# Moving the second batch's bucket products and value halves, and loading two weight chunks into an idle buffer

## The chip, the cores and the metric

The kernel runs on one core of one Trainium2 chip. Its engines are TensorE (PE, with its weight loads PEld), VectorE (DVE), ScalarE (ACT), GpSimd (POOL) and SyncE (SP), which issues nearly all transfers. The metric is the device time of one launch in microseconds (us); lower is better.

## The reference

Hash-bucketed attention is followed by two feed-forward layers.

- Attention: batch 2, 8 heads, 768 positions, head width 64. Six signs of a projection give each query and key a bucket number; a query attends only to keys of its own bucket: `softmax(where(q_bucket == k_bucket, q @ k.T / 8, -1e9)) @ v`.
- First layer, on 1536 tokens of width 512: `h = x @ w_in` (512 to 2048), `g = where(h > 0, h, exp(min(h, 0)) - 1)`, `x = g @ w_out` (2048 to 512).
- Second layer: `h = x @ w_in2`, `g = s * max(h, 0)**2 + b`, `out = g @ w_out2`, of the same sizes.

The weights arrive as 64-bit floats, the inputs of attention as 32-bit floats.

## The kernel before

**Precision.** Products run on 16-bit pairs: each operand is split into a high half and a low half (the rest), and a product is three matmuls: high by high, high by low, low by high.

**Weights of the first layer.** `w_stream` is a generator that works on chunks of 512 KB raw 64-bit data. A step of it does four things: it finishes the chunk that was joined one step before (L188 on ACT writes the high half, L204 on DVE or L202 on POOL the low half), joins the oldest loaded chunk from its two 32-bit words into a float (L194, L195, L197 on DVE), and issues the load of the next chunk (L167, on SP's queue) into one of three raw buffers. A join waits until two chunks are in `loaded`, so a chunk is loaded two steps before it is joined; 16 chunks need 19 steps. `w_in` is streamed in the first loop of attention (L823), one step a yield from unit 2 on. `w_out` gets its own generator behind it (L844); it is stepped by `w1_step` in the loop over the first layer's slots (two slots of three, L873). Its chunks come by column group: four for each of the four 128-column groups of `w_out`. Before unit 40's scores the stream has to be through: `att_step` drains it (L860). At its end its buffers are given to attention.

**Attention** is 96 units (batch, 128 queries, head): 48 of each batch. A unit is: scores on PE (L358), clamp and row minimum on DVE (L368), exponential on ACT (L370), then a split into halves (L389 on ACT, L392 on POOL), a transposing transfer `pt<-ph` on SP's queue (L394), and the product with the values on PE (L412), some four units later. Eight units make a chunk of 128 tokens, which `u_norm` writes to the input `xx` of the first layer. `xx` is three tiles of four chunks: `xx[1]` first gets data behind unit 39.

**Set-up of batch 1.** Heads go in pairs `hp` 0 to 3. While units 41 to 54 run, four functions are called at steps written out by hand (`sched`, by unit number): `p_split` (halves of k and q and their transposes) at unit 41 + 2 hp, `p_bits` (signs: 20 matmuls L320, then L323 on DVE) three units later, `p_buck` (four matmuls L333, then four activations L337 that write the bucket part of k and q) one unit after that. `p_v` splits the values: L303 on ACT, L304 on DVE. The first scores of pair `hp` in batch 1 are unit 48 + 2 hp, and the first product with its values is that unit's L412.

**Order.** The program text gives priorities. From them and its own timeline of the engines the framework's planner writes one fixed order for each engine and each queue, in which the chip executes. The first layer's products (L531) lie between attention's steps. It runs in blocks of 256 tokens: `up` 16 slots (`h`), `down` 16 slots (`x2p`). The second layer (`h` again, then `y` L775) follows when attention is over.

Of the kernel before, what the change touches and what calls it, by code (L numbers as in the profile page):

```python
# [10 lines left out]
I32 = mybir.dt.int32  # L11
# [30 lines left out]
WST = 2  # L42
LOAD1 = [30, 41, 42, 44]
LOADV1 = [46, 46, 48, 48]
PV1 = [48, 49, 50, 52]

GUEST = [(0, "k"), (0, "q"), (2, "k"), (2, "q"), (0, "v"), (1, "v")]
NS = 2
# [13 lines left out]
SC_N = 16  # L62
PRE = 4
W_FROM = 2
LN2 = 0.6931471805599453


def model_kernel(tc, q, k, v, proj, w_in, w_out, w_in2, w_out2, s2, b2, sel, pop, eye, out):
    nc = tc.nc
# [23 lines left out]
    with ExitStack() as base:  # L93
# [50 lines left out]
        def w_raw(st):  # L144
            return pool(st, "wraw", WRAW, side="right")


        def w_tiles(p, nm):
            return [p.tile([128, KF, 512], F16, name=f"{nm}{x}") for x in "hl"]

        def w_in_chunks(dst, dram):
            w = dram.bitcast(I32)
            return [((lambda a, f=f: dst(f)) if callable(dst) else [d[:, f, :] for d in dst], w[:, 256 * f:256 * f + 256].rearrange("(k p) n -> p k n", p=128))
                    for f in range(KF)]

        def w_col_chunks(dst, dram):
            w = dram.bitcast(I32)
            return [([z[:, f:f + 4, 128 * d:128 * d + 128] for z in dst],
                     w[128 * f:128 * f + 512, 256 * d:256 * d + 256].rearrange("(k p) n -> p k n", p=128))
                    for d in range(KM) for f in range(0, KF, 4)]  # L160

        def w_load(ch, wraw):
            t = wraw.tile([128, 512, 2], I32, tag="w", name="wraw")
            o = t.rearrange("p n t -> p (n t)")
            if len(ch[1].shape) == 3:
                o = o.rearrange("p (k n) -> p k n", k=ch[1].shape[1])
            nc.sync.dma_start(out=o, in_=ch[1])  # L167
            return t

        def w_stream(chunks, wraw, words, delay=0, aside=0):  # L170
            loaded, joined = [], []
            for n_, ch in enumerate(chunks + [None] * 3):
                with late_by(delay):
                    done = joined.pop(0) if joined else None
                    if done:
                        (dst, _), w = done
                        w = w.bitcast(F32)
                        if callable(dst):
                            dst = dst(w)
                            done = dst and (None, w)  # L180
                    if done:
                        hi, lo = dst
                        if len(hi.shape) == 3:
                            w = w.rearrange("p (k n) -> p k n", k=hi.shape[1])
                        aside_ = n_ - 3 < aside
                        if aside_:
                            nc.gpsimd.tensor_scalar(w, w, SW, None, op0=ALU.mult)
                        nc.scalar.activation(out=hi, in_=w, func=ACTF.Copy, scale=1.0 if aside_ else SW)  # L188
                    if len(loaded) == 2 or (ch is None and loaded):
                        c0, t = loaded.pop(0)  # L190
                        a, x = words()
                        a, x = a.bitcast(I32), x.bitcast(I32)
                        low, top = t[:, :, 0], t[:, :, 1]
                        nc.vector.tensor_scalar(x, top, 3, 0x3FFFFFFF, op0=ALU.logical_shift_left, op1=ALU.bitwise_and)  # L194
                        nc.vector.scalar_tensor_tensor(out=x, in0=low, scalar=29, in1=x,  # L195
                                                       op0=ALU.logical_shift_right, op1=ALU.bitwise_or)
                        nc.vector.scalar_tensor_tensor(out=a, in0=top, scalar=-0x40000000, in1=x,  # L197
                                                       op0=ALU.bitwise_and, op1=ALU.bitwise_or)
                        joined.append((c0, a))
                    if done:  # L200
                        if aside_:
                            nc.gpsimd.tensor_tensor(out=lo, in0=w, in1=hi, op=ALU.subtract)  # L202
                        else:
                            nc.vector.scalar_tensor_tensor(out=lo, in0=w, scalar=SW, in1=hi,  # L204
                                                           op0=ALU.mult, op1=ALU.subtract)
                    if ch is not None:
                        loaded.append((ch, w_load(ch, wraw)))
                yield
# [153 lines left out]
        def u_soft(u):  # L362
# [5 lines left out]
            nc.vector.tensor_scalar(f, sps.pop(u), CLAMP, None, op0=ALU.min, op1=ALU.min, accum_out=mx)  # L368
            (nc.gpsimd if U0 <= u < MXP else nc.vector).tensor_scalar(mx, mx, sm / (SQ * SQ), 10.0 * LN2, op0=ALU.mult, op1=ALU.add)  # L369
            nc.scalar.activation(out=f, in_=f, func=ACTF.Exp, scale=-sm / (SQ * SQ), bias=mx,  # L370
# [44 lines left out]
        xx = [xs_.tile([128, 2 * KM, 512], F16, name=f"x{i}") for i in range(B * C // 4)]  # L415
# [28 lines left out]
        def at(step, fn, *a):  # L444
            sched.setdefault(step, []).append((fn, a))
# [10 lines left out]
        for hp in range(HP):  # L456
            at(PV0 + hp, p_v, 0, hp)
            e1 = (C - 1) * H + 2 * hp + 1
            at(LOAD1[hp], p_load, 1, hp, "k")
            at(LOAD1[hp], p_load, 1, hp, "q")  # L460
            at(e1, p_split, 1, hp, "k", "act")
            at(e1, p_split, 1, hp, "q", "act")
            at(e1 + 3, p_bits, 1, hp)
            at(e1 + 4, p_buck, 1, hp)
            at(LOADV1[hp], p_load, 1, hp, "v")
            at(PV1[hp], p_v, 1, hp)
        done_chunks = [0]
        in_done = [0]
        nxt = {"s": 0, "av": 0, "soft": [], "split": [], "lag": LAG0}
# [339 lines left out]
        if True:  # L809
# [3 lines left out]
            for hp, nm in ((0, "k"), (0, "q"), (1, "k"), (1, "q")):  # L813
# [5 lines left out]
            wdec = w_raw(wdst), lambda: (wst.tile([128, 512], F32, tag="wa", name="wa"),  # L819
                                         ring.take("w", [128, 512], F32, "wx"))  # L820
            ws1 = w_stream(w_in_chunks(wi, w_in), *wdec, aside=ASIDE)
            n = 0
            for _ in att:  # L823
                n += 1
                if nxt["s"] >= W_FROM and n % WN == 0:
                    next(ws1, None)
                if done_chunks[0] == BLOCKS1[0]:
                    break
# [12 lines left out]
                gp[0] = pool(gst1, "gp1", 1)  # L841

            wo = w_tiles(wop, "wo")
            ws1 = chain(ws1, w_stream(w_col_chunks(wo, w_out), *wdec))  # L844
            live = {"w1": True, "att": True}
            credit = 0.0

# [24 lines left out]
            for ks, cost in enumerate(moe1(wi, wo, gp, next_gp, tmp, tmpg, att_step)):  # L872
# [7 lines left out]
                if not live["att"] and ws2 is None:  # L880
                    exst.close()
                    ast.close()
                    ps_y = pool(pst, "ps_y", Y2, space=PSUM)
                    lp = right(late, "late", 1)
                    tmp2.append(right(late, "tmp2", 3))
                    wraw = w_raw(wlate)
                    wjp = right(wlate, "wjoin", 1)
                    sbt = lp.tile([128, 2], F32, name="sbt")
                    sbs = const.tile([128, 3], F32, name="sbs")
                    nc.sync.dma_start(out=sbt[:, 0:1], in_=s2.rearrange("(o t) -> o t", o=1).to_broadcast([128, 1]))  # L890
                    nc.sync.dma_start(out=sbt[:, 1:2], in_=b2.rearrange("(o t) -> o t", o=1).to_broadcast([128, 1]))
                    nc.vector.tensor_scalar(sbs[:, 0:1], sbt[:, 0:1], UN * SG2, None, op0=ALU.mult)
                    nc.vector.tensor_scalar(sbs[:, 1:2], sbt[:, 1:2], SG2, None, op0=ALU.mult)
                    nc.vector.tensor_scalar(sbs[:, 2:3], sbt[:, 1:2], 2.0 * SG2, None, op0=ALU.mult)
                    sb["s"], sb["b"], sb["2b"] = (sbs[:, x:x + 1] for x in range(3))
                    wq = []
                    co = wo_chunks(w_out2, wq, wjp)
                    ci = w_in_chunks(wi2_new, w_in2)
                    ch = ci[:W2PRE]
                    for f in range(KF):  # L900
                        ch += ci[W2PRE + f:W2PRE + f + 1] + co[f:f + 1]
                    ws2 = w_stream(ch, wraw,
                                   lambda: (wjp.tile([128, 512], F32, tag="wa", name="wa", bufs=4),
                                            ps_x.tile([128, 512], F32, tag="x", name="wx")), delay=D2)
                elif ws2 is not None and W2EV(ks) and fed2[0] < W2PRE + 3:
                    next(ws2)
                    fed2[0] += 1
# [72 lines left out]
```

## Time and profile before

| | |
|---|---|
| median of 3 runs | 716.36 us (713.94 to 717.16) |
| profiled execution: time, span | 715.27 us, 713.5 us |
| mean granted TensorE clock | 0.986 of full speed |
| chunks of `w_out` finished | 16, from 108.8 to 179.9 us |
| set-up of batch 1 | 180.6 to 248.5 us |

The share of the chain of work that ended last is 59% PE, 11% transfers, 10% ACT, 7% DVE. Read the profile by stretches: an engine's share over the whole span mixes a first part, in which attention's dependencies set the pace, with a second in which PE has no idle time. A wait's row names what came last.

### The profile page before, as it was taken

How to read it: one execution, taken by the hardware profiler on the slowest of the kernel's cores; microseconds unless marked ns; L12 is line 12 of the kernel's file. 1: busy time of each engine (PE TensorE's matmuls, PEld its weight loads, DVE VectorE, ACT ScalarE, POOL GpSimd, SP SyncE). 2: the span in 40 equal slices, each digit the busy share in tenths (PEclk: the TensorE clock that was granted, in tenths of full speed). 3: DMA queues.
4: the chain of work that ended last, by engine and by line, in shares of the span. 5: the costliest groups of instructions: out<-in, count | busy, mean ns of one | idle time of the engine just before them, and what ended most of it. 6: DMA issues, size and time to landing. Idle time of an engine off the chain costs nothing.

```text
span 713.5 us, 15214 instructions
## 1 busy us (share of the span) xinstructions
PE 659.6 (92%) x6192; PEld 504.0 (71%) x6192; DVE 516.6 (72%) x885; ACT 417.2 (58%) x687; POOL 272.7 (38%) x219
## 2 busy tenths in 40 slices
PE   2789869888887999999999999999999999999998
PEld 0368657676666777888888988874444446888887
DVE  5688899888878468645744699439999726999730
ACT  2897679874797887756755333234555525555520
POOL 1257778873445278945854421311211200000000
PEclk9999979999999999999999999999999999999999
DMA  9984599999899588966768545004453000000100
GB/s 234 259 222 135 159 223 225 205 229 219 178 208 215 88 142 159 154 119 123 123 112 120 132 153 175 1 25 125 121 149 115 0 1 1 16 30 32 45 30 30
DMA packets 206742, 89.73 MB, mean 126 GB/s; under 512 B 171856, under 2 KB 203344, under 8 KB 206672
## 3 DMA queue, kind: packets, MB, share of 16 engines
q1 hardware_dynamic: 206080, 88.63, 56.4%
q8 instruction: 48, 0.79, 0.5%
q10 hardware_dynamic: 592, 0.14, 0.1%
q14 instruction: 22, 0.18, 0.1%
HBM read 43.13 MB, written 3.15 MB: 65 GB/s over the span
## 4 chain that ended last, share of the span: by engine, by line
PE 59%; DMA 11%; ACT 10%; DVE 7%; issue 6%; POOL 5%; SPq 0%; DVEq 0%; ACTq 0%; POOLq 0%
PE h L531 24%; PE y L775 15%; PE x2p L531 10%; DMA pt<-ph 6%; PE s L358 4%; POOL ph L392 3%; ACT p L370 3%; PE xacc L412 3%; ACT ph L389 2%; PE xacc L406 1%; DVE e L546 1%; DMA k<-src 1%; ACT gh L551 1%; PE pT L379 1%; DVE p L368 1%
## 5 line engine op out<-in xcount | busy, mean ns | idle before, releaser
L392 POOL TENSOR_TENSOR ph<-p,ph 128x768 f16<-128x768 f32 x80 | 133.9, 1679 | 65.3 <-ACT ph L389 45.7
L531 PE MATMUL h<-x,wih 128*128 128x256 f16 x768 | 132.5, 276 | 0.1
L531 PE MATMUL h<-x,wi 128*128 128x512 f16 x576 | 124.5, 379 | 0.0
L368 DVE TENSOR_SCALAR_CACHE_REDUCE p<-s 128x768 f32<-128x768 f32 x96 | 91.0, 950 | 44.4 <-PE s L358 42.1
L370 ACT ACTIVATE p<-p,mx 128x768 f32<-128x768 f32 x96 | 89.1, 928 | 46.4 <-DVE mx L369 40.5
L775 PE MATMUL y<-wqh,a 128*128 128x256 f16 x672 | 110.3, 273 | 0.0
L775 PEld LDWEIGHTS <-a 128*128 128x128 f16 x1008 | 98.5, 98 | 11.8
L531 PE MATMUL x2p<-gh,woh 128*128 128x256 f16 x384 | 104.8, 274 | 2.0 <-ACT woh L188 1.0
L531 PE MATMUL x2p<-gh,wol 128*128 128x256 f16 x384 | 105.0, 274 | 1.5 <-DVE wol L204 1.5
L531 PE MATMUL h<-x,wil 128*128 128x256 f16 x384 | 106.0, 276 | 0.0
L531 PE MATMUL x2p<-gl,woh 128*128 128x256 f16 x384 | 104.9, 274 | 0.5 <-POOL gl L554 0.4
L531 PEld LDWEIGHTS <-wi 128*128 128x128 f16 x576 | 56.3, 98 | 67.8
L775 PE MATMUL y<-wql,a 128*128 128x256 f16 x336 | 91.2, 273 | 0.0
L358 PE MATMUL s<-k,q 128*128 128x512 f16 (+1 forms) x384 | 81.0, 336 | 4.8 <-DVE p L368 4.5
L531 PEld LDWEIGHTS <-woh 128*128 128x128 f16 x768 | 74.8, 98 | 13.5 <-ACT woh L188 1.4
L531 PEld LDWEIGHTS <-wih 128*128 128x128 f16 x768 | 75.2, 99 | 12.8 <-issue 0.5
L554 POOL TENSOR_TENSOR gl<-g,gh 128x512 f16<-128x512 f32 x48 | 58.1, 1211 | 63.3 <-ACT gh L551 62.7
L412 PE MATMUL xacc<-vv,pt 128*128 128x64 f16 x1440 | 57.7, 195 | 18.2 <-DMA pt<-ph 18.2
L412 PEld LDWEIGHTS <-pt 128*128 128x128 f16 x1440 | 53.9, 99 | 24.3 <-DMA pt<-ph 21.2
L389 ACT ACTIVATE ph<-p 128x768 f16<-128x768 f32 x80 | 66.6, 836 | 5.2 <-DMA pt<-ph 4.1
L567 DVE SCALAR_TENSOR_TENSOR g<-h,sbs,r 128x512 f32<-128x512 f32 x48 | 35.7, 745 | 23.6 <-ACT r L564 23.6
L564 ACT ACTIVATE r<-h 128x512 f32<-128x512 f32 x48 | 28.2, 590 | 39.5 <-PE h L531 39.5
(121 smaller groups left out, 1043.3 us busy)
## 6 DMA issues: line engine op xcount, KB each, us to landing
wraw<-in_moe_w_in SPq DMA_DIRECT2D x32, 512.0 KB, 3.8
wraw<-in_moe_w_out SPq DMA_DIRECT2D x32, 512.0 KB, 3.9
out<-y SPq DMA_DIRECT2D x10, 256.0 KB, 2.0
raw<-in_k SPq DMA_DIRECT2D x6, 384.0 KB, 4.4
raw<-in_q SPq DMA_DIRECT2D x6, 384.0 KB, 4.4
v<-in_v SPq DMA_DIRECT2D x4, 384.0 KB, 5.1
pt<-ph SPq DMA_TRANSPOSE x80, 4.0
x<-in_k SPq DMA_DIRECT2D x2, 384.0 KB, 5.0
```

Of the source, the lines that this page charges most:

```text
L358: nc.tensor.matmul(p[:, a0:a1], w[b, hp][:, j, c, :], kf[:, a0:a1], start=(x == 0), stop=(x == 1))
L368: nc.vector.tensor_scalar(f, sps.pop(u), CLAMP, None, op0=ALU.min, op1=ALU.min, accum_out=mx)
L370: nc.scalar.activation(out=f, in_=f, func=ACTF.Exp, scale=-sm / (SQ * SQ), bias=mx, accum_out=sums[b, c][:, h:h + 1])
L379: nc.tensor.transpose(p[:, 128 * cc:128 * cc + 128], f[:, 128 * cc:128 * cc + 128], ident)
L389: nc.scalar.activation(out=t[:, 0, :], in_=f, func=ACTF.Copy)
L392: nc.gpsimd.tensor_tensor(out=t[:, 1, :], in0=f, in1=t[:, 0, :], op=ALU.subtract)
L412: nc.tensor.matmul(acc, o[:, C * x + cc, :], vv[:, j, cc, y, :], start=(z == 0 and cc == 0), stop=(z == 2 and cc == C - 1))
L531: nc.tensor.matmul(p, ws[a](kk), xs[b](kk), start=(kk == 0 and z == 0), stop=(kk == n_kk - 1 and z == 2))
L554: nc.gpsimd.tensor_tensor(out=gl, in0=t["g"], in1=gh, op=ALU.subtract)
L564: nc.scalar.activation(out=t["r"], in_=p, func=ACTF.Relu, scale=UN)
L567: nc.vector.scalar_tensor_tensor(out=g, in0=p, scalar=sb["s"], in1=t["r"], op0=ALU.mult, op1=ALU.mult)
L775: nc.tensor.matmul(p, a[:, xa, kk, :], wq[y][:, WQ[n], kk, :], start=first and k == 0, stop=k == 3 * K2 - 1, skip_group_check=True)
```

## The change

Four things change: `BUCK1`, a new constant, puts `p_buck` of batch 1 two units behind `p_bits`, not one. `PV1` calls `p_v` of pairs 1 to 3 at units 50, 52 and 54, not 49, 50 and 52; pair 0 stays at 48. In the first loop of attention the raw data of the first two chunks of `w_out` is loaded into `xx[1]`, at units 6 and 8 (one tile of `xx` holds just two raw chunks). The stream of `w_out` then starts with these two in `loaded`: its first step joins at once, and it has 17 steps, not 19. Since `wo` does not exist yet when the early loads are issued, the chunks' destinations become functions.

```diff
-PV1 = [48, 49, 50, 52]
+PV1 = [48, 50, 52, 54]
+BUCK1 = 5
+EARLY = [6, 8]
...
+        def w_early(ch, x):
+            t = xx[1].rearrange("p a t -> p (a t)").bitcast(I32)[:, 1024 * x:1024 * x + 1024]
+            nc.sync.dma_start(out=t.rearrange("p (k n) -> p k n", k=ch[1].shape[1]), in_=ch[1])
+            return ch, t.rearrange("p (n t) -> p n t", t=2)
+
-        def w_stream(chunks, wraw, words, delay=0, aside=0):
-            loaded, joined = [], []
+        def w_stream(chunks, wraw, words, delay=0, aside=0, loaded=(), late_dst=False):
+            loaded, joined = list(loaded), []
...
+                        if late_dst:
+                            dst = dst()
...
-            at(e1 + 4, p_buck, 1, hp)
+            at(e1 + BUCK1, p_buck, 1, hp)
...
-            n = 0
+            n, early = 0, []
+            co1 = w_col_chunks(lambda: wo, w_out)
             for _ in att:
                 n += 1
+                if len(early) < len(EARLY) and nxt["s"] >= EARLY[len(early)]:
+                    early.append(w_early(co1[len(early)], len(early)))
...
-            ws1 = chain(ws1, w_stream(w_col_chunks(wo, w_out), *wdec))
+            ws1 = chain(ws1, w_stream(co1[len(early):], *wdec, loaded=early, late_dst=True))
```

## Rows read from the trace of the kernel before

**Rows 1.** The page: busy time of each engine over the span.
```profile
PE 659.6 (92%) x6192; PEld 504.0 (71%) x6192; DVE 516.6 (72%) x885; ACT 417.2 (58%) x687; POOL 272.7 (38%) x219
```
**Rows 2.** Busy time by stretches; first columns: stretch, its length.
```profile
core 0: us, PE busy (x) PEld busy (x) DVE busy (x) ACT busy (x) POOL busy (x), PEclk, DMA share, GB/s
...
100.00:162.00 62.00, 56.27 (x679) 46.31 (x678) 55.09 (x98) 51.02 (x93) 48.62 (x47) 0.96 1.07 225
162.00:181.00 19.00, 16.47 (x203) 13.50 (x202) 15.88 (x26) 7.83 (x13) 5.13 (x4) 1.00 0.92 217
181.00:245.00 64.00, 54.62 (x617) 42.07 (x616) 47.08 (x83) 52.59 (x87) 30.89 (x23) 0.97 0.91 176
...
300.00:445.00 145.00, 144.49 (x1657) 125.96 (x1656) 93.10 (x182) 76.78 (x130) 70.05 (x50) 1.00 0.65 133
```
**Rows 3.** PE's waits, 165 to 185 us: total, times, longest.
```profile
PE x2p L531 <- DVE wol L204: 1.5, 3, 0.9
PE x2p L531 <- ACT woh L188: 1.0, 2, 0.7
```
**Rows 4.** DVE's instructions by line, 162 to 181 us: busy, mean ns, idle before.
```profile
L204 DVE SCALAR_TENSOR_TENSOR wol<-wa,woh 128x512 f16<-128x512 f32 x6 | 5.2, 871 | 2.8 <-ACT woh L188 2.8
L194 DVE TENSOR_SCALAR wx<-wraw 128x512 int32<-128x512 int32 x5 | 3.5, 693 | 0.1
```
**Rows 5.** SP's queue in order of time, two places: start, length.
```profile
41.33 18.10 SPq L167 DMA_DIRECT2D wraw<-in_moe_w_in  x4
...
98.07 0.38 SPq L167 DMA_DIRECT2D wraw<-in_moe_w_out  x1
```
**Rows 6.** Busy time by stretches, 40 to 60 us.
```profile
40.00:60.00 20.00, 17.67 (x140) 14.56 (x140) 15.25 (x32) 17.25 (x28) 11.24 (x9) 0.91 0.58 187
```
**Rows 7.** PE's waits, 185 to 250 us.
```profile
PE xacc L412 <- DMA pt<-ph: 5.1, 6, 1.3
PE pone L333 <- DVE bits L323: 2.3, 1, 2.3
```
**Rows 8.** All engines in order of time, around pair 2's bucket products.
```profile
226.73 3.27 DVE L304 SCALAR_TENSOR_TENSOR vv<-x,vv 128x768 f16<-128x768 f32 x2
226.97 4.53 POOL L392 TENSOR_TENSOR ph<-p,ph 128x768 f16<-128x768 f32 x2 [0.49 <-ACT ph L389]
...
229.93 0.94 DVE L323 TENSOR_SCALAR bits<-pbit 128x768 f16<-128x768 f32 x1
...
230.93 0.80 PE L333 MATMUL pone<-bits,sel_sb 128*128 128x512 f16 x2 [2.33 <-DVE bits L323]
```
**Rows 9.** Busy time by stretches, 231 to 234.2 us.
```profile
231.00:234.20 3.20, 3.20 (x14) 1.91 (x14) 2.39 (x6) 0.73 (x1) 0.50 (x1) 0.50 1.09 133
```
**Rows 10.** DVE in order of time: clamps of units 45, 46, 51 and 52.
```profile
194.50 0.94 DVE L368 TENSOR_SCALAR_CACHE_REDUCE p<-s 128x768 f32<-128x768 f32 x1
...
208.49 0.95 DVE L368 TENSOR_SCALAR_CACHE_REDUCE p<-s 128x768 f32<-128x768 f32 x1
...
241.40 0.95 DVE L368 TENSOR_SCALAR_CACHE_REDUCE p<-s 128x768 f32<-128x768 f32 x1
...
248.07 0.96 DVE L368 TENSOR_SCALAR_CACHE_REDUCE p<-s 128x768 f32<-128x768 f32 x1 [0.70 <-PE s L358]
```
**Rows 11.** ACT in order of time: last bucket activations of pairs 0 and 3.
```profile
205.77 1.80 ACT L337 ACTIVATE q<-pone,pop_sb 64x768 f16<-64x768 f32 x2
...
246.67 1.80 ACT L337 ACTIVATE q<-pone,pop_sb 64x768 f16<-64x768 f32 x2
```
**Rows 12.** PE in order of time: scores of units 48 and 54.
```profile
219.49 0.81 PE L358 MATMUL s<-k,q 128*128 128x512 f16 x4
...
250.36 0.81 PE L358 MATMUL s<-k,q 128*128 128x512 f16 x4
```
**Rows 13.** Tile vv, 185 to 250 us: least, median, greatest ns.
```profile
L304 DVE SCALAR_TENSOR_TENSOR vv<-x,vv x2: 958/1679/2400, 226.7 to 227.6; 128x768 f16<-128x768 f32 x2
L304 DVE SCALAR_TENSOR_TENSOR vv<-raw,vv x2: 957/958/958, 232.4 to 239.7; 128x768 f16<-128x768 f32 x2
```

More of the change, by code (lines that the diff above doesn't have):

```diff
@@ L157, in w_col_chunks @@
             w = dram.bitcast(I32)
-            return [([z[:, f:f + 4, 128 * d:128 * d + 128] for z in dst],
+            return [((lambda d=d, f=f: [z[:, f:f + 4, 128 * d:128 * d + 128] for z in dst()]),
                      w[128 * f:128 * f + 512, 256 * d:256 * d + 256].rearrange("(k p) n -> p k n", p=128))
```

## The prediction

> **What bounds the kernel now.** I read the page's busy shares first, then stretches, then PE's waits in the stretches that the change touches, then the order of time around them. PE is busy 92% of the span [rows 1], and the stretches show where the rest lies: from 300 to 445 us it is idle 0.5 of 145 us, so nothing is to be had there from an earlier attention. From 100 to 162 us it is idle 5.7 of 62 us, from 162 to 181 us 2.5 of 19, from 181 to 245 us 9.4 of 64 [rows 2]. PE's work is the same after the change, so the change is worth the idle time and slow clock that it takes out of these three stretches, or puts in.
>
> In the first of them DVE is the fullest engine beside PE: 55.1 of 62 us. In the second the picture turns: DVE 15.9 of 19, ACT 7.8, POOL 5.1 [rows 2]. That is the drain of `w_out`'s stream ahead of unit 40's scores: five chunks are joined one behind the other (five of L194, and five each of its two companions L195 and L197; six of L204), with 2.8 us of waiting for ACT's high half inside [rows 4]. Attention stands still meanwhile. In the third, attention starts batch 1, in long chains over all engines, and PE's fixed order runs into them.
>
> **The early loads.** They remove no work: 16 chunks are loaded, joined and split as before. Two loads move from just before the stretch at 100 us, where the second of them is issued at 98.07, to units 6 and 8, that is into the time when SP itself sat 18.1 us over four loads, waiting for raw buffers [rows 5]. The early loads wait for no buffer, but they stand in SP's queue behind such a load, and what is queued behind them (the next `w_in` loads, the transposes of the first chunks of `xx`) starts one issue later. An issue takes 0.38 us [rows 5], so two cost at most 0.8 us if all of it fell on the path; transfers are at a share of 0.58 from 40 to 60 us [rows 6], so the data fits beside the rest. I take 0 and keep 0 to +0.8 for the range.
>
> What they do change is the stream's start: the first join comes in step 1, not step 3. Every chunk is finished two steps sooner in the program, three slots of the first layer. Where the drain starts, 13 chunks are done instead of 11, and three are left instead of five. A chunk costs DVE three joins of 0.69 us (the row of L194; three instructions alike) and 0.69 to 0.87 us of L204 [rows 4], about 2.8 us; so the drain loses 5.6 us of DVE time, which turns up between 100 and 162 us. There DVE has 6.9 us idle [rows 2], so it fits at best wholly into gaps, at worst not at all, and attention enters the drain between 0 and 5.6 us later and leaves it between 5.6 and 0 us earlier than now. PE's own gain is smaller. In the drain PE has products to do and stops only for the weights themselves: 1.5 + 1.0 = 2.5 us [rows 3]. With three chunks less to wait for (the last column group is needed at slot 28, and its last chunk comes at slot 25 instead of 28 in the program's order) these waits go. What is late next is attention's restart, which PE reaches 2.5 us sooner: the gain holds if attention leaves the drain at least 2.5 us earlier, about the middle of the 0 to 5.6 us above. I take **-2.5 us**, with ends -2.5 (all kept) and 0 (handed on to the first transposes of batch 1).
>
> **Bucket products one unit later, value halves one or two units later.** No instruction is added. Of the 64 us from 181 on I look at the one long wait of PE that these functions make: pair 2's bucket product waits 2.33 us for its signs. The signs (L323) stood on DVE behind two value halves (L304), which took 3.27 us together [rows 8]. With `p_v` of pair 1 at unit 50, at least one of these two is behind the signs, and with `p_buck` a unit later the product comes into PE's order when its signs are ready. So 2.3 us go [rows 7], **-2.3**. The wait has a tail: right behind it the granted clock is 0.50, the lower level of 1.2 GHz, over 3.2 us [rows 9], which costs PE half of 3.2 us, **-1.6**.
>
> Against that stands what waits for the bucket activations: the scores of the same pair. Now pair 0's last activation ends at 205.77 + 1.80 = 207.57 us [rows 11] and its first scores (unit 48) start at 219.49 [rows 12], a margin of 11.9 us. A unit later is 14.0 us there (clamps of units 45 and 46 at 194.50 and 208.49 [rows 10]), so PE would wait 2.1 us. Pair 3 ends at 248.47 [rows 11] and unit 54 starts at 250.36 [rows 12], a margin of 1.9; a unit there is 6.7 us (units 51 and 52 at 241.40 and 248.07 [rows 10]), which would be a wait of 4.8 us. Bounds for this new wait: 0 if the planner finds first-layer products to put before the scores, 2.1 + 4.8 = 6.9 us if it finds none. I take **+2.1**: pair 0's unit is long whatever the change does, whereas pair 3's unit is long because of the chain in [rows 8] that gets shorter, and `down` products are there to fill it.
>
> The three moved value halves have their readers from unit 50 on, some four units behind the scores, and their raw data lies in buffers that nothing else wants in batch 1; I cost the move itself at 0. If that cover were gone, one ACT and one DVE instruction of 0.96 us [rows 13] would stand before a product, under 2 us. One of the four L304 took 2.40 us and the others 0.96 [rows 13], the long one beside two splits on POOL of 4.53 us together [rows 8]. The Trainium skill (SBUF — State Buffer, Who interferes with whom) says that a VectorE instruction with two inputs in SBUF and a GpSimd instruction that reads SBUF shut each other out of a shared port; the row agrees. By that rule three moved halves could each lose or gain 2.40 - 0.96 = 1.44 us of DVE time, by where they land beside POOL's splits; the sum here takes none of it.
>
> **Sum.** -2.5 - 2.3 - 1.6 + 2.1 = -4.3 us. The profiled execution took 715.27 us (its span 713.5 and 1.8 around it), so 711.0; the median of the runs shown is 716.36, 1.1 above it, which gives **712.1 us** as a median. A measurement of this kernel can tell about 0.5%, 3.6 us: faster begins at 712.8, slower at 719.9.
>
> **The rivals.**
>
> *The waits move on.* PE's order is fixed against a chain of transfers: six waits for the transposes `pt<-ph`, 5.1 us, stand in the same stretch [rows 7]. If attention leaves the drain no earlier, each us saved in front of one of these comes back behind it: 716.4 us, give or take 2. For it speaks that DVE's work from 100 to 181 us is the same sum; against it that DVE waited idle inside the drain for 2.8 us [rows 4], a loss that shrinks with it.
>
> *More than the named waits.* If attention does restart 5.6 us earlier, the planner's order for batch 1 has that much more slack, and other idle time of the 9.4 us goes too. Half of what is left beyond the 2.3 already counted is 3.5 us: with -2.5 - 2.3 - 1.6 and no new wait this is -9.9, 705.4 in the profile and 706.5 as a median. For it speaks that this stretch has the most idle time after 100 us; against it that its chains are latencies, which an earlier start alone doesn't shorten.
>
> *The late bucket.* The scores take over the wait: pair 0 and pair 3 both lose their margin, 6.9 us, and behind the second wait the clock falls as in [rows 9], 1.6 us more; in return -3.9 as above, and the drain's 2.5 us are eaten by the wait behind it. 715.27 - 3.9 + 6.9 + 1.6 = 719.9, or 721.0 as a median. It decides from the point where the activations end later than the planner's place for the scores by more than 1.9 us in pair 3. For it speaks that this margin is smaller than any unit in the stretch; against it that the planner sees this dependency and reorders.
>
> That the change doesn't do what it says can be ruled out for the loads' number, but the planner may leave a moved step where it was; this is part of the first rival.
>
> **How the numbers follow.** Forecast 0.42, waits move on 0.18, more than the named waits 0.16, late bucket 0.24. The forecast's own range is 709 to 716 (its median 712.1, with the drain's gain at 0 to the upper side and the new wait at 0 or 4.8 to either). It counts as faster in 0.72 of its cases and as the same in the rest: 0.30 and 0.12. The second rival is wholly faster, 0.16; the first the same in 0.13, faster in 0.01, slower in 0.04; the late bucket slower in 0.20, the same in 0.04. Together: faster 0.47, same 0.29, slower 0.24. The range goes from below the second rival's 706.5 to the late bucket's 721.0: 705 to 721, with the 0.8 us of the early issues inside.
>
> **What would show it.** Right: two loads of `w_out` between 41 and 85 us; three chunks back to back in the drain and no wait of `x2p` for `woh` or `wol` over 0.5 us; attention's first split of batch 1 before 178 us instead of 181; no wait of L333 over 1 us and no stretch at 0.50 between 200 and 250 us; a new wait of L358 for L337 of about 2 us. Wrong: DVE idle from 100 to 162 us still near 6.9 us although its work grew (then attention was pushed, not filled); PE's idle time from 181 to 245 us at 9 us or more; or a wait of L358 for L337 over 4 us.

## The result: slower by 1.1%, and the profile after

The changed kernel takes 722.24 us (median of 4 runs, 720.71 to 723.46) where the kernel before, run beside it, takes 715.25 (4 runs). The ratio on record is 1.0114, with a 95% interval of 1.0083 to 1.0145; the quotient of the two medians, 1.0098, lies inside it. The forecast was 712.1 us and its range went from 705 to 721. The profiled execution took 723.46 us, 8.2 more than that of before.

First the page's busy line, against [rows 1]. The kernel's lines have moved: those from L187 to L820 of before stand 9 further down here (the low half L204 is now L213, its counterpart on POOL L202 is L211, the multiply L187 is L196, the signs' product L333 is L342).

```profile
PE 665.2 (92%) x6192; PEld 507.9 (70%) x6192; DVE 516.8 (72%) x883; ACT 417.6 (58%) x687; POOL 275.0 (38%) x223
```

The counts hold the surprise. The prediction had "They remove no work" of the early loads and "No instruction is added" of the rest. DVE has 883 where it had 885, and POOL 223 where it had 219: two instructions have left DVE and four have come to POOL. The groups of POOL between 100 and 185 us show which (line, engine, operation, tiles, count, then busy us, mean ns, idle us before them):

```profile
L196 POOL TENSOR_SCALAR wa<-wa 128x512 f32<-128x512 f32 x2 | 3.0, 1488 | 0.2
L211 POOL TENSOR_TENSOR wol<-wa,woh 128x512 f16<-128x512 f32 x2 | 2.3, 1159 | 0.2
```

Two chunks of `w_out` are now split by way of POOL: POOL multiplies the joined words (L196), ACT makes the high half from the product, and POOL subtracts (L211). Before, no chunk of `w_out` went that way. The reason stands in one line of `w_stream` that the diff does not touch: `aside_ = n_ - 3 < aside`, with `n_` the stream's step. It means "the first `aside` chunks go over POOL"; `w_in` asks for some, and `w_out` for none, `aside=0`. A chunk used to be finished in step 3 at the earliest (steps count from 0), so `n_ - 3` began at 0. With two chunks loaded beforehand, the first two are finished in steps 1 and 2; `n_ - 3` is -2 and -1, which is less than 0, and both take the detour.

The stretches, against [rows 2] (us; busy time and instructions of PE, PEld, DVE, ACT, POOL; granted TensorE clock, DMA share, GB/s):

```profile
100.00:162.00 62.00, 54.77 (x639) 43.96 (x637) 57.59 (x92) 50.54 (x90) 49.02 (x46) 0.94 0.98 202
162.00:181.00 19.00, 18.59 (x223) 14.85 (x221) 17.99 (x27) 10.99 (x19) 10.35 (x10) 0.94 1.11 226
181.00:245.00 64.00, 56.08 (x568) 43.09 (x572) 44.13 (x83) 48.86 (x82) 25.14 (x21) 0.89 0.94 180
245.00:300.00 55.00, 51.11 (x653) 41.89 (x653) 35.51 (x78) 42.75 (x75) 39.41 (x27) 1.00 0.83 137
300.00:445.00 145.00, 144.66 (x1683) 126.04 (x1681) 90.85 (x182) 79.83 (x136) 74.16 (x52) 1.00 0.66 130
```

The fourth stretch is not among [rows 2]; before it was

```profile
245.00:300.00 55.00, 53.36 (x671) 44.61 (x670) 39.50 (x86) 45.67 (x82) 42.40 (x29) 1.00 0.90 146
```

PE's idle time has hardly changed in sum: 7.2 us in the first stretch (5.7 before), 0.4 in the second (2.5), 7.9 in the third (9.4), 3.9 in the fourth (1.6). The clock has: 0.94, 0.94 and 0.89 in the first three (0.96, 1.00 and 0.97 before). I took all stretches of one us from 40 to 320 us and added up two things: PE's idle time, and its busy time multiplied by what the granted clock is short of full speed. Before they are 30.8 and 8.1 us, after 31.6 and 15.9. The sum grows by 8.6 us, about the 8.2 of the two executions, and nearly all of it is clock. That isn't one execution's accident: the mean granted clock is 0.969 to 0.976 in all four executions of the changed kernel, and 0.973 to 0.993, on average 0.984, in those of the kernel before that ran beside the experiments (one of 984 us, far out of line, is left out here and in the ratios).

Not all of the 8.2 us need be the change's, though. A part is there by 65 us, long before the detour. The clamp of unit 10 (units count from 0), before, after, and in experiment e6 below:

```profile
62.21 0.96 DVE L368 TENSOR_SCALAR_CACHE_REDUCE p<-s 128x768 f32<-128x768 f32 x1 [0.31 <-PE s L358]
...
64.85 0.96 DVE L377 TENSOR_SCALAR_CACHE_REDUCE p<-s 128x768 f32<-128x768 f32 x1 [0.37 <-PE s L367]
...
67.06 0.96 DVE L377 TENSOR_SCALAR_CACHE_REDUCE p<-s 128x768 f32<-128x768 f32 x1 [0.37 <-PE s L367]
```

After is 2.6 us late there. But e6 runs the order of before on PE, DVE, ACT and POOL up to 170 us and is 4.9 us late, and e2, with that order up to 195 us, is 2.4 us early (59.78). Executions of one order differ that much, so the 2.6 us may belong to this execution; single profiles below are to be read with this in mind.

Three pairs of stretches show how the clock comes in, the wait and what follows it (columns as above; in the second and third pair the two overlap):

```profile
144.00:147.00 3.00, 0.64 (x20) 0.63 (x20) 3.00 (x6) 1.20 (x3) 2.70 (x3) 1.00 1.25 233
147.00:151.00 4.00, 4.00 (x35) 2.46 (x32) 4.00 (x10) 3.70 (x8) 3.45 (x3) 0.57 1.23 185
...
188.00:193.00 5.00, 2.00 (x27) 1.16 (x25) 3.62 (x9) 5.00 (x10) 3.03 (x3) 0.85 1.03 192
191.00:199.00 8.00, 7.08 (x62) 4.44 (x60) 7.56 (x14) 6.27 (x12) 5.71 (x5) 0.57 1.08 234
...
212.00:215.00 3.00, 0.39 (x7) 0.11 (x6) 0.69 (x1) 2.06 (x5) 1.15 (x1) 1.00 1.38 147
214.00:219.00 5.00, 4.10 (x34) 2.96 (x35) 3.36 (x6) 3.10 (x6) 3.86 (x4) 0.66 1.11 217
```

Each time PE first runs 0.4 to 2.0 us in 3 to 5, and then works, with under 1 us of idle time, through 4 to 8 us whose mean clock is 0.57 or 0.66: most of it is at the lower level (0.5, which is 1.2 GHz). PE's waits, in the same order, are 2.36 us for a transpose, 2.08 for the transfer `k<-src` with 0.92 for `x` behind it, and 2.61 for a transpose.

### The profile page after: what moved, and what is told of

Same layout as the page of the kernel before. It is cut to its first block, busy times and chain, and to the rows that moved or that the text cites. A ratio compares the mean times of both kernels' runs of the same rounds, so it can differ in the third digit from the quotient of the medians.

```text
span 721.7 us, 15215 instructions
## 1 busy us (share of the span) xinstructions
PE 665.2 (92%) x6192; PEld 507.9 (70%) x6192; DVE 516.8 (72%) x883; ACT 417.6 (58%) x687; POOL 275.0 (38%) x223
## 4 chain that ended last, share of the span: by engine, by line
PE 58%; DMA 8%; DVE 7%; issue 3%; ACT 3%; POOL 2%; SPq 0%; DVEq 0%; ACTq 0%; POOLq 0%
PE h L540 25%; PE y L784 15%; PE x2p L540 11%; DMA pt<-ph 6%; PE s L367 3%; PE xacc L421 3%; DVE p L377 1%; DVE e L555 1%; POOL ph L401 1%; ACT ph L398 1%; DVE wol L213 1%; DVE g L557 1%; DVE wa L206 1%; POOL gl L563 1%; ACT gh L560 1%
## 5 line engine op out<-in xcount | busy, mean ns | idle before, releaser
L401 POOL TENSOR_TENSOR ph<-p,ph 128x768 f16<-128x768 f32 x80 | 132.2, 1656 | 78.2 <-ACT ph L398 53.5
L540 PE MATMUL h<-x,wih 128*128 128x256 f16 x768 | 135.2, 278 | 1.0 <-DVE x L633 0.9
L377 DVE TENSOR_SCALAR_CACHE_REDUCE p<-s 128x768 f32<-128x768 f32 x96 | 91.1, 952 | 45.6 <-PE s L367 42.0
L367 PE MATMUL s<-k,q 128*128 128x512 f16 (+1 forms) x384 | 83.3, 343 | 5.0 <-DVE p L377 4.0
L421 PE MATMUL xacc<-vv,pt 128*128 128x64 f16 x1440 | 59.2, 196 | 21.0 <-DMA pt<-ph 21.0
L367 PEld LDWEIGHTS <-q 128*128 128x128 f16 x384 | 35.4, 102 | 24.0 <-issue 9.5
```

What stands on the lines that cost most here:

```text
L367: nc.tensor.matmul(p[:, a0:a1], w[b, hp][:, j, c, :], kf[:, a0:a1], start=(x == 0), stop=(x == 1))
L401: nc.gpsimd.tensor_tensor(out=t[:, 1, :], in0=f, in1=t[:, 0, :], op=ALU.subtract)
L421: nc.tensor.matmul(acc, o[:, C * x + cc, :], vv[:, j, cc, y, :], start=(z == 0 and cc == 0), stop=(z == 2 and cc == C - 1))
L540: nc.tensor.matmul(p, ws[a](kk), xs[b](kk), start=(kk == 0 and z == 0), stop=(kk == n_kk - 1 and z == 2))
```

## The experiments

All were timed in five rounds against the kernel before, which ran beside them at 713.8 to 714.4 us. Ratios are to that; brackets hold the 95% interval.

**e1, the early loads alone.**

```diff
-PV1 = [48, 50, 52, 54]
-BUCK1 = 5
+PV1 = [48, 49, 50, 52]
+BUCK1 = 4
 EARLY = [6, 8]
```

> The early loads alone, with the old places of the bucket products and value halves. The traces of before and after reach the same amount of matmul work 3.8 us apart at 185 us and 8.2 us apart at the end. Theory 1 (the early stream costs before the set-up of batch 1, the late buckets behind it): +3.8 us against before, about 719 us. Rival 2 (all of it is the early stream, and the rest only its echo in batch 1): +7 to +8, about 723. Rival 3 (all of it is the late buckets): 0, about 715.

Measured: 721.11 us, 1.0096 [1.0064, 1.0127]. The loads with what hangs on them are enough for nearly all of the loss.

**e2, the late functions alone** (`EARLY = []`, the rest as changed).

> The late bucket products and value halves alone, without early loads. Theory 1: the part behind 185 us, +4.4 us, about 719.7. Rival 2: 0 within 1 us. Rival 3: +7 to +8, about 723. The forecast on record had this part at -1.8 us (-2.3 -1.6 +2.1), about 713.5.

Measured: 717.11 us, 1.0037 [1.0013, 1.006]. A loss where the prediction saw -3.9 and +2.1.

**e3, the early loads without the detour**, and **e4, the whole change without it.**

```diff
-                        aside_ = n_ - 3 < aside
+                        aside_ = bool(aside) and n_ - 3 < aside
```

> As the early loads alone, but the first two chunks of w_out are finished by DVE as in before. In the changed kernel they go through GpSimd (a multiply and a subtraction each), because the test for it counts steps from the stream's start and the stream now starts two steps further on. Theory 4 (that detour, 5.3 us of GpSimd work and low halves on DVE that take 1.45 us beside it instead of 0.85, is what the early stream costs after 100 us): what remains is the 2.6 us lost by 60 us, of which little is left at 134 us: 0 to +2.6 us against before, 715 to 718. Rival 5 (the loads themselves, or the joins two steps sooner, are the cost): the same as the early loads alone, within 1 us.

> The whole change, with the first two chunks of w_out finished by DVE as in before. Theory 4 with theory 1: the late part's +4.4 us and at most 2.6 of the early one: 719 to 722. Rival 5: as the changed kernel, 722. If the forecast on record failed by the detour alone: 711 to 713.

Measured: e3 715.33 us, 1.0014 [0.9994, 1.0035]; e4 714.05 us, 0.9995 [0.9972, 1.0017]. The detour makes 5.8 us of e1's time (721.11 - 715.33) and 8.2 of the change's (722.24 - 714.05; these two ran in different rounds, and each against its own kernel before they are 7.2 apart). Without it the change is worth nothing.

**e5, the detour alone**, in the kernel before: `aside` becomes a set of chunks, and `w_out`'s chunks 0 and 1 are in it. Nothing is loaded early or moved. **e6, the same detour elsewhere:** chunks 12 and 13, in the drain.

```diff
-                        aside_ = n_ - 3 < aside
+                        aside_ = n_ - 3 in aside
...
-            ws1 = chain(ws1, w_stream(w_col_chunks(wo, w_out), *wdec))
+            ws1 = chain(ws1, w_stream(co1[len(early):], *wdec, aside=(0, 1), loaded=early, late_dst=True))
```

> The kernel before, with nothing of the change but the detour: chunks 0 and 1 of w_out are finished over GpSimd (multiply and subtraction). No early loads, the stream has its 19 steps. Theory 4 (the detour is the cost: 5.3 us of work on a GpSimd that is busy 48.6 of 62 us there, in front of the splits that attention's row buffers wait for): +5 to +7 us against before, as far as the early loads alone lie above those finished by DVE (5.8). Rival 6 (the detour costs only together with the stream that starts two steps sooner, or the reshuffled order does): 0 to +2.

> The kernel before with the same detour for chunks 12 and 13 instead, which are finished in the drain ahead of unit 40, where GpSimd is busy 5.1 of 19 us. Theory 4: no cost, -1.5 to +1 us against before. Rival 6 (any reshuffling of the planned order costs some us): +3 to +6, here as for chunks 0 and 1.

Measured: e5 719.09 us, 1.006 [1.0037, 1.0084]; e6 714.70 us, 1.0008 [0.9982, 1.0034]. The same four instructions on POOL cost 4.3 us (0.6% of 714.35) among attention's splits and nothing that can be measured in the drain. What happens among the splits is seen at POOL's queue in the changed kernel (start us, us, engine, line, operation, tiles):

```profile
110.97 1.49 POOL L196 TENSOR_SCALAR wa<-wa 128x512 f32<-128x512 f32 x1
112.54 1.69 POOL L401 TENSOR_TENSOR ph<-p,ph 128x768 f16<-128x768 f32 x1
...
117.43 1.49 POOL L196 TENSOR_SCALAR wa<-wa 128x512 f32<-128x512 f32 x1
119.00 1.16 POOL L211 TENSOR_TENSOR wol<-wa,woh 128x512 f16<-128x512 f32 x1
120.51 1.65 POOL L401 TENSOR_TENSOR ph<-p,ph 128x768 f16<-128x768 f32 x1
...
123.96 1.16 POOL L211 TENSOR_TENSOR wol<-wa,woh 128x512 f16<-128x512 f32 x1
```

L401 is attention's split. From a chunk's multiply to its subtraction pass 8.0 us for the first chunk and 6.5 for the second: weights and attention take turns in one queue. DVE at the same time:

```profile
116.26 0.96 DVE L377 TENSOR_SCALAR_CACHE_REDUCE p<-s 128x768 f32<-128x768 f32 x1
...
120.19 0.69 DVE L206 SCALAR_TENSOR_TENSOR wa<-wraw,wx 128x512 int32<-128x512 int32 x1 [1.07 <-POOL wol L211]
...
126.39 2.00 DVE L213 SCALAR_TENSOR_TENSOR wol<-wa,woh 128x512 f16<-128x512 f32 x1
...
128.91 0.94 DVE L377 TENSOR_SCALAR_CACHE_REDUCE p<-s 128x768 f32<-128x768 f32 x1
```

The join of the third chunk (L206) waits 1.07 us until POOL's subtraction gives one of the two joined buffers free. And the two clamps (L377), those of units 26 and 27, are 12.65 us apart. In the kernel before the same two are 7.28 us apart:

```profile
113.80 0.95 DVE L368 TENSOR_SCALAR_CACHE_REDUCE p<-s 128x768 f32<-128x768 f32 x1
...
121.08 0.95 DVE L368 TENSOR_SCALAR_CACHE_REDUCE p<-s 128x768 f32<-128x768 f32 x1
```

In e1, e5 and e9 (below) the gap is 12.7, 12.7 and 11.1 us, in e3 and e6 6.5 and 7.2. Waiting is the smaller part of the longer gap: DVE is idle 2.27 us in it (0.78 before). It also has 12 instructions to run between the two clamps where it had 8. Unit 27's clamp stands further back in the order that the planner wrote around POOL's new work.

**e7, the bucket products alone** (`EARLY = []`, `BUCK1 = 5`, `PV1` as before), and **e8, the values alone** (`EARLY = []`, `BUCK1 = 4`, the new `PV1`).

> The bucket products one unit later, the value halves at their old places. The late part as a whole gave +2.6 us (0.37%). If the buckets are what costs in it: +2.6, 1 to 4. If it is the value halves: 0 within 1 us.

> The value halves of pairs 1 to 3 later, the bucket products at their old place. The planned order differs from before's in a few instructions of DVE and ACT and between PE's matmuls alone. If the buckets are what costs in the late part: 0 within 1 us; the forecast on record would have it take away the 2.3 us wait of the third pair's product and the clock behind it, -2 to -4. If the value halves cost: +1 to +4.

Measured: e7 717.26 us, 1.0043 [1.0021, 1.0066]; e8 713.87 us, 0.9996 [0.9971, 1.0021].

e8 tells less than it was meant to, since the planner left the values where they were. By operation and tile, the order on PE, DVE, ACT and POOL is that of the kernel before. Both value halves still run ahead of pair 2's signs (L332):

```profile
226.43 3.28 DVE L313 SCALAR_TENSOR_TENSOR vv<-x,vv 128x768 f16<-128x768 f32 x2
229.63 0.94 DVE L332 TENSOR_SCALAR bits<-pbit 128x768 f16<-128x768 f32 x1
```

and PE still waits 2.4 us for the signs. The new `PV1` makes no difference between e7 and e2 either: both run one order (sign products aside, which run side by side on PE). So they are two measurements of it, and the loss of both is the bucket products'. In e7, the matmuls around pair 2's product show it, against [rows 8] and [rows 9] (in square brackets: idle us before it, and what ended that):

```profile
233.73 0.27 PE L540 MATMUL x2p<-gl,woh 128*128 128x256 f16 x1 [2.73 <-POOL gl L563]
...
234.95 0.67 PE L342 MATMUL pone<-bits,sel_sb 128*128 128x512 f16 x2 [0.62 <-DVE p L377]
```

and the stretch behind:

```profile
235.00:238.50 3.50, 3.50 (x17) 2.42 (x17) 0.08 (x1) 3.39 (x6) 0.40 (x1) 0.52 1.01 202
```

The product's own wait fell from 2.33 to 0.62 us. Right ahead of it a product of the first layer now waits 2.73 us for POOL, and the stretch behind is at 0.52: wait and slow clock are still there, under another name. But they only replace what was there before, and so they aren't e7's loss. Its stretches:

```profile
181.00:245.00 64.00, 54.44 (x602) 41.95 (x600) 47.33 (x85) 51.73 (x86) 30.12 (x23) 0.97 0.93 178
245.00:300.00 55.00, 53.00 (x683) 44.22 (x679) 38.28 (x81) 44.60 (x78) 41.28 (x28) 1.00 0.82 140
300.00:445.00 145.00, 143.17 (x1643) 124.78 (x1642) 93.27 (x183) 77.49 (x132) 69.65 (x49) 1.00 0.63 131
```

PE is idle 9.6 us in the first (9.4 before, at the same clock), and 3.8 in the other two together (2.1 before); in e2 it is 9.5 and 4.0. What the late products cost shows up behind the set-up of batch 1.

**e9, the multiply alone:** chunks 0 and 1 are multiplied on POOL as in e5, but DVE makes the low half.

```diff
-                        if aside_:
+                        if aside_ and not late_dst:
                             nc.gpsimd.tensor_tensor(out=lo, in0=w, in1=hi, op=ALU.subtract)
+                        elif aside_:
+                            nc.vector.scalar_tensor_tensor(out=lo, in0=w, scalar=1.0, in1=hi,
+                                                           op0=ALU.mult, op1=ALU.subtract)
```

> The kernel before with half of the detour: chunks 0 and 1 of w_out are multiplied on GpSimd (2 x 1.49 us of the 5.3), and their low halves are written by DVE. If the detour costs by GpSimd's time in front of attention's splits: its share, 4.3 x 3.0 / 5.3 = +2.4 us against before. If it costs because DVE's next join waits for GpSimd's subtraction to free the joined buffer (1.1 us in the traces): 0 to +1.

Measured: 719.22 us, 1.007 [1.0039, 1.0102]. The two subtractions, 2.3 us of POOL, add nothing that can be seen; two multiplies are enough for e5's whole loss. Its profile can't say where: of the 5.9 us by which this execution is behind, 4.2 are there at unit 10's clamp (66.45 us), ahead of the multiplies.

**e10, loads that nobody reads:** two loads of the early loads' size into `xx[1]` at units 6 and 8; the stream of `w_out` stays as before.

> The kernel before, plus the two early loads into the idle tile of xx at units 6 and 8, whose data nobody reads: the stream loads the same chunks again in its own time, with 19 steps and no detour. It is the price of the two early transfers alone. If they are hidden, as the forecast on record had it: 0 to +0.8 us. If the 2.6 us by which the changed kernel is behind at 60 us are theirs: +1.5 to +3.

Measured: 713.99 us, 0.9997 [0.9975, 1.002].

**e11, e3 with the new `PV1`,** to see whether the drain's earlier end is worth something when the values make room.

> The change without its two costly parts: early loads with their chunks finished by DVE, value halves later, bucket products at their old place. From the early loads finished by DVE (+1.1 us) and the values alone (-0.5): +0.6 us, within 1.5 of before. If taking the drain's waits away is worth what the forecast on record said (-2.5): 711 to 713.

Measured: 714.89 us, 1.0017 [0.9991, 1.0042]. It isn't; but here too the planner left the values where they were. e11 runs the order of e3 (1.0014) and measures it a second time.

**e12, POOL's time without the chain:** the kernel before with e9's two multiplies at e9's places in POOL's order, but their result goes to the idle `xx[1]` and nobody reads it.

```diff
                             dst = dst()
+                            if n_ - 3 in (0, 1):
+                                z = xx[1].rearrange("p a t -> p (a t)").bitcast(F32)[:, 1024 * (n_ - 3):1024 * (n_ - 3) + 512]
+                                nc.gpsimd.tensor_scalar(z, w, SW, None, op0=ALU.mult)
```

> The kernel before with two extra GpSimd multiplies of 128x512, of the joined words of w_out's chunks 0 and 1 into the idle buffer of xx: nobody reads their result. They stand at the same places of GpSimd's order as the two multiplies of e9, but the high half is made from the joined words by ACT alone, as before, and the low half by DVE: neither waits for GpSimd. Theory chain (what costs 5 us in e9 is that the high half, the low half and with them one of the two joined buffers wait for a multiply that stands behind attention's splits in GpSimd's queue): as before, ratio 0.998 to 1.002 (about 714 us), the gap between the clamps of units 26 and 27 at 7 us. Rival, GpSimd's time (two times 1.49 us in the queue that attention's splits use, just where the splits follow one another): ratio 1.005 to 1.008 as in e5 and e9 (718 to 719.5 us), that gap at 11 to 13 us. In between, with the gap at 7 us, it would be the order that the planner makes of the rest.

Measured: 716.56 us, 1.0031 [1.0011, 1.0051], or 2.2 us. The two clamps (L380 in this kernel):

```profile
116.72 0.95 DVE L380 TENSOR_SCALAR_CACHE_REDUCE p<-s 128x768 f32<-128x768 f32 x1
...
127.55 0.94 DVE L380 TENSOR_SCALAR_CACHE_REDUCE p<-s 128x768 f32<-128x768 f32 x1
```

They are 10.8 us apart. Neither theory is met: the gap is there although the high half waits for no multiply, but the loss is half of e9's. Between the clamps DVE again has 12 instructions, here and in e9, and waits for POOL in neither, so the gap is made by the order that the planner wrote around POOL's time. The other half of the loss would be the chain's, by difference. The intervals of e9 (1.0039 to 1.0102) and e12 overlap, and a joined buffer still comes free only when POOL has read it, so this split is likely and not shown.

## Why the prediction was wrong

**The step that failed** is the first sentence on the early loads: "They remove no work: 16 chunks are loaded, joined and split as before." Loaded and joined, yes. Two of them are split otherwise, over POOL. I read the diff for what it moves, and did not ask who else uses the step number `n_` whose meaning it shifts. Undoing only this takes the change from 1.0114 back to 0.9995 (e4); putting it alone into the kernel before costs 4.3 us (e5).

That takes away the loss and leaves no gain: the forecast, 712.1 against 716.36, is a ratio of 0.994, below e4's interval. **The gains failed by themselves.** -2.5 was handed on to later waits, the -2.3 and -1.6 came back behind other waits, and one sentence under them was false: "With `p_v` of pair 1 at unit 50, at least one of these two is behind the signs". In the changed kernel, as in e8, both value halves still stand ahead of pair 2's signs on DVE, at 223.86 and 227.37 us:

```profile
227.37 0.96 DVE L313 SCALAR_TENSOR_TENSOR vv<-x,vv 128x768 f16<-128x768 f32 x1 [1.89 <-ACT vv L312]
...
230.03 0.95 DVE L332 TENSOR_SCALAR bits<-pbit 128x768 f16<-128x768 f32 x1
```

The prediction had named this case ("the planner may leave a moved step where it was"), as a part of its first rival.

How four instructions of together 5.3 us, on an engine that is 38% busy, cost this much is the second lesson. POOL was busy 48.6 of 62 us in that stretch already before, with attention's splits among its work, and behind the splits come the transposes for which PE waits. The planner makes room for the new work by writing unit 27's clamp further back, and attention is 5 us later from there to the drain. A loss need not be idle time: in the two profiled executions it is in the clock in the changed kernel (15.9 against 8.1 us), whereas in e5 PE's idle time grows from 30.8 to 35.6 us and the clock's part falls from 8.1 to 7.0. Whether PE pays by waiting or by a lower clock behind its waits seems to depend on how the waits fall.

**Early loads, their issue** (0, bounds 0 to +0.8): right. e10 is at 0.9997, and e3 within 0.2% as well. (An early load's issue took 0.51 us, not 0.38.)

**The waits in the drain, -2.5:** the waits went, the time did not. (The drain has two chunks fewer, from five to three; "three chunks less" is a slip.) In the changed kernel, against [rows 3]:

```profile
PE x2p L540 <- DVE wol L213: 0.2, 1, 0.2
PE x2p L540 <- ACT woh L197: 0.2, 1, 0.2
```

There the detour confuses the picture, so take e3, which is free of it. The same two waits are 0.7 us together, and attention's restart behind the drain, POOL's first step after its long idle time, is 1.95 us earlier:

```profile
179.84 0.19 POOL L378 TENSOR_SCALAR mx<-mx 128x1 f32<-128x1 f32 x1 [9.14 <-DVE p L377]
```

Before, the line is

```profile
181.79 0.19 POOL L369 TENSOR_SCALAR mx<-mx 128x1 f32<-128x1 f32 x1 [11.86 <-DVE p L368]
```

(and 185.60 us in the changed kernel). Yet e3 is at 1.0014. In its stretches

```profile
162.00:181.00 19.00, 17.94 (x216) 14.82 (x216) 17.12 (x31) 9.60 (x16) 6.15 (x7) 1.00 0.95 209
181.00:245.00 64.00, 54.76 (x607) 42.45 (x606) 44.56 (x78) 52.76 (x87) 30.89 (x22) 0.95 0.96 182
245.00:300.00 55.00, 52.40 (x665) 43.71 (x663) 39.48 (x84) 42.93 (x77) 40.31 (x28) 1.00 0.81 141
```

PE's idle time goes from 2.5 to 1.1 us in the first, stays in the second (9.4 and 9.2, at a clock of 0.95) and grows from 1.6 to 2.6 us in the third. That is the rival "The waits move on", for this part of the change: what is saved ahead of batch 1's chains comes back inside them. That the planner would use the earlier start ("More than the named waits") is out: e3, e4 and e11 gain nothing.

**The product's wait, -2.3, and the clock behind it, -1.6:** "the product comes into PE's order when its signs are ready" looked at one of two things that the product needs. The wait for the signs did go, as in e7, where the later place is all that changed. In the changed kernel pair 2's signs end at 230.98, 6.7 us before its product. But the product is written into one of the buffers of PE's results that the scores take too (`p_buck` asks for `tag="s"`, the scores' tag), and so it waits 1.51 us for a clamp that reads scores:

```profile
237.67 0.48 PE L342 MATMUL pone<-bits,sel_sb 128*128 128x512 f16 x2 [1.51 <-DVE p L377]
```

The clamp stands on DVE behind two copies of q (L304 in this kernel; the median of its 12 on DVE is 0.36 us):

```profile
233.82 2.80 DVE L304 COPY q<-q 64x768 f16<-64x768 f16 x2 [1.26 <-DMA q<-src]
236.65 0.96 DVE L377 TENSOR_SCALAR_CACHE_REDUCE p<-s 128x768 f32<-128x768 f32 x1
```

The stretch behind the wait, which was to lose its slow clock:

```profile
239.00:243.00 4.00, 3.81 (x32) 2.82 (x33) 1.37 (x5) 3.38 (x6) 0.00 (x0) 0.57 0.29 64
```

So one of the prediction's signs of being right, no wait over 1 us and no stretch at 0.50 between 200 and 250 us, is missing, while none of its signs of being wrong is there: they didn't foresee this way of failing. In e7 the product's 0.62 us are a wait for a clamp as well, and in e4 it waits 1.8 us for one, so this part is not the detour's. That the shared buffers are the cause rests on the code and on the instruction that the trace names; no run gave the product buffers of its own.

**The scores' new wait, +2.1:** not there. No row of PE's waits from 185 to 270 us has the scores waiting for bucket activations, neither in the changed kernel nor in e7; in e4 there is one of 0.5 us, but e5, with the products at their old place, has one too. So "The late bucket", the rival on the slower side, foretold a loss in the right functions by the wrong mechanism. e7's 3.1 us (0.43% of 714) aren't in a wait for the activations; 1.7 us of idle time stand behind 245 us, and what causes them was not found. The prediction allowed that the planner would fill in front of the scores (its bound 0), and it did.

**The values, 0:** the number is right (e8, 0.9996), by luck: nothing moved, so the cover of some four units that it was argued from was never tested. The **port**: the low half of `w_out` (two inputs in SBUF) between 100 and 185 us

```profile
L204 DVE SCALAR_TENSOR_TENSOR wol<-wa,woh 128x512 f16<-128x512 f32 x16 | 13.6, 848 | 2.8 <-ACT woh L188 2.8
```

takes 848 ns on average before, and in the changed kernel

```profile
L213 DVE SCALAR_TENSOR_TENSOR wol<-wa,woh 128x512 f16<-128x512 f32 x14 | 19.3, 1377 | 0.7 <-ACT woh L197 0.7
```

1377 ns: 14 instructions take 5.7 us more than 16 did. The Trainium skill (SBUF — State Buffer, Who interferes with whom) has VectorE's second SBUF input and GpSimd's reads share one interface, and the rows agree: the two that no work of POOL overlaps (181.02 and 183.73 us) take 0.69 us, and the longest, beside a split, takes 2.15. But that isn't the loss: in e3 the same 16 take 17.6 us (1100 ns on average), 4.0 more than before, and e3 costs nothing that can be measured.

**What stays open.** The detour costs 4.3 us in the kernel before (e5), 5.8 with the early loads (e1 against e3) and 8.2 in the whole change (after against e4). The bucket products cost 3.1 us in the kernel before (e7) and nothing on top of e3 (e4 against e3). By the runs' intervals the first three can't be told apart with certainty, but the last two can, so there the parts don't add up. A likely reason is that each of these edits makes the planner write another order from there on; no run adds the detour or the late products with the rest of the order held fixed. A joined buffer more, which would free the chain without moving the detour, wasn't tried.

## What to carry to other kernels

When a change shifts the start of a counted loop, search for every other use of the counter before you price anything, and compare the instruction counts of each engine first when the result comes in: two less on DVE and four more on POOL pointed to the cause at once. Compare the order of each engine too: three runs here moved a step in the program that the planner left where it was. A wait that disappears is only worth its time if what stands behind it was late because of it. In a stretch of long chains with a fixed order, price it at zero until a run shows otherwise. Work on a half-idle engine is not free where it shares a queue with the chain that feeds the bound engine: the same four instructions cost 4 us among attention's splits and nothing in the drain.

## What the runs showed of the hardware

In the profiled executions PE's clock made more of this result than its idle time. In the changed kernel each of the three waits of 2.08 to 2.61 us from 140 to 250 us has a stretch at the lower level behind it, which costs PE another 1.4 to 3.0 us (busy time times what the clock is short: 4.10 x 0.34 and 7.08 x 0.43). It is no rule of the idle time alone: in the same kernel PE runs 0.86 of 3 us from 251 to 254 us, and the clock is 1.00 there and from 254 to 256 us.

```profile
251.00:254.00 3.00, 0.86 (x21) 0.65 (x20) 1.05 (x4) 2.88 (x6) 1.62 (x1) 1.00 1.31 120
254.00:256.00 2.00, 2.00 (x32) 1.75 (x31) 0.00 (x0) 1.98 (x4) 0.02 (x1) 1.00 0.47 88
```

So of two executions with the same idle time (30.8 and 31.6 us from 40 to 320 us) one can lose 8 us more to the clock, and a forecast that prices waits by their length has that much of uncertainty in it. A single profile has some too: executions of one order were 2.4 us early to 4.9 us late at 62 us.
